# Gate-value products in PSUM, early weight operands and stored token operands in a fused attention and two-MLP kernel

## The chip, the cores and the metric

The kernel runs on one core of a Trainium2 chip. Its metric is the device time of one launch in microseconds, the median of several runs. Beside it stands the profiled execution, one run recorded by the hardware profiler; all rows below come from that one execution.

The engines are named as the profile names them: PE (TensorE, matmuls), PEld (its weight loads), DVE (VectorE), ACT (ScalarE), POOL (GpSimd) and SP (SyncE, here the queue that issues nearly all DMAs). PSUM is the memory that PE writes, eight banks of 128 partitions by 512 fp32 numbers; SBUF is the working memory, and DRAM lies behind the DMA queues.

## The reference, cut to what matters

```
state = 0                                     # a recurrence over 768 tokens, 4 batches x 8 heads, head size 48
y[t]  = r[t] @ (state + u * k[t] v[t]^T);  state = w[t] * state + k[t] v[t]^T
x  = y, laid out as 3072 tokens x 384
h  = max(x @ w1, x @ w2, x @ w3)              # first MLP, 384 -> 768
x  = h @ w_out                                # 768 -> 384
g, val = x @ w_gate, x @ w_val                # second MLP, 384 -> 1536, gated
out = (g * sigmoid(g) * val) @ w_out2         # 1536 -> 384
```

Everything is in fp32. The kernel reaches that accuracy with matmuls of the rounded type fp32r: each operand is split into a high and a low part, and one exact product is three matmuls (high x high, high x low, low x high; `mm3`, lines 618 to 621, and the loop in `product`, lines 926 and 927).

## The kernel before, in words

The 3072 tokens are six chunks of 512 (`NT`). The kernel has two halves.

First half: the attention of chunk c (24 units, `group` and its helpers) is computed beside the first MLP of chunk c-1 (`up`, `down`). PE does 18 `up` groups and three `down` results a chunk. The result goes to DRAM (`y1d`). The weights of the second MLP come in as 64-bit words and are turned to fp32 beside it (`bits`, chunks 8 to 19) and stored in `wfd`.

Second half, the gated MLP: three pairs of chunks (d = 0 to 2) times four quarters of the 1536 hidden features (q) make twelve units, n = 4d + q. A unit needs, for the gate (v = 0) and for the value (v = 1), the products of three weight blocks with three token blocks for two chunks, 18 block products; a fast scheme makes them from 15 (`ORD`, `CHAIN`). Each of the 15 is three matmuls of 128x128 by 128x512. So both operands are sums:

- token side, once a pair d: `y_sum` (POOL, 11 sums), `op_high` (ACT, rounding) and `op_low` (the remainder, DVE, for the indices in `SLOW` on POOL). The 15 results `op[d, r]` lie in one buffer each, so the operand i of the next pair can be written only when product i of the value side of the last unit of this pair has run.
- weight side, once a quarter q, in units 0 to 3: `w_sum` (POOL), `w_high` (ACT), `w_low` (DVE, parts of it POOL). The result is used at once and stored (`w_store`) for the units 4 to 11, which load it (`w_load`). The weights of the projection go the same way (`p_high`, `p_low`, `p_store`, `p_load`). Seven buffers `u0` to `u6` hold the parts in a ring (`WSLOT`).

What follows a product: PE accumulates into six PSUM chains (letters A to F in `CHAIN`; A and B use the two banks `gx`, the others a ring of four banks, `mm`). `snap` (ACT) copies a chain to SBUF, `join` (DVE) adds the chain's new state to such a copy, `mix` (POOL) adds two copies. After that `silu` (ACT, gate), `times` (DVE, gate by value, in SBUF), `prod_high` (ACT) and `prod_low` (DVE or POOL) give the operand of the projection. `proj` (PE, nine matmuls each, six a unit) uses two PSUM banks `po` and `collect` adds its result to an accumulator (ACT for the first quarter of a pair, else DVE). The six projections of unit n stand between the products of unit n+1 (`seq`, the table `gaps`: after products 10 and 13 of the gate side and 2, 6, 9 and 12 of the value side). A unit is 90 matmuls of products and 54 of projections.

The order of all work is made by a list scheduler (`Plan`), which gives each engine a fixed list from the costs, due times and dependencies written in the code; SP's list of DMAs comes out of the same plan. At run time each engine goes through its list in order and waits for what each entry needs. `close` (line 1044) marks the point at which the attention's buffers are given up and those of the second half come into being.

Of the kernel before, what the change touches and what calls it, by code (L numbers as in the profile page):

```python
# [20 lines left out]
C = 128  # L21
# [18 lines left out]
class Plan:  # L40
# [4 lines left out]
    SLOTS = 4  # L45
# [5 lines left out]
    def add(self, eng, cost, fn, deps=(), due=None, lat=0.1, slot=0, after=0.0, slack=0.0, kind=0):  # L51
        t = dict(kind=kind, eng=eng, cost=cost, fn=fn, deps=[d for d in deps if d is not None], due=due, lat=lat,
                 slot=slot, after=after, slack=slack, readers=[], id=len(self.items), start=None, end=None)
        self.items.append(t)
        return t
# [6 lines left out]
    def order(self):  # L62
# [21 lines left out]
        free, last, dma, slots, out = {}, {}, 0.0, [], []  # L84
# [3 lines left out]
        while avail:  # L88
            best = None
            for t in avail:  # L90
# [3 lines left out]
                if t["slot"] and len(slots) + t["slot"] > self.SLOTS:  # L94
                    held = [r for o, i in slots[-self.SLOTS:][:t["slot"]] for r, part in o["readers"] if part in (None, i)]
# [19 lines left out]
            t["end"] = t["start"] + t["cost"]  # L115
            free[t["eng"]] = t["end"]
# [3 lines left out]
            slots += [(t, i) for i in range(t["slot"])]  # L120
# [156 lines left out]
def fused(ctx: ExitStack, tc: tile.TileContext, pk, ub, wt_all, out):  # L277
# [10 lines left out]
           for q in range(NQ)]  # L288
    wpd = [dram.tile([128, 2, 9, C], F32, name=f"wpd{q}") for q in range(NQ)]
# [14 lines left out]
    psM = tail.enter_context(tc.tile_pool(name="psM", bufs=4, space=PSUM))  # L304
# [28 lines left out]
    for t, v in ((signs, 0.0), (small, 1.0), (tiny, -TINY), (blo, W_LO), (bhi, -W_HI), (one, 1.0)):  # L333
        nc.gpsimd.memset(t, v)

# [100 lines left out]
    def rk_sum(n):  # L436

        pas[n] = psM.tile([128, 8], F32, tag="mm", name="pa")
# [41 lines left out]
    def transposes(n):  # L480
        khT[n] = psM.tile([128, G, C], F32, tag="mm", name="kp")
# [228 lines left out]
    def up(c, f, m):  # L710
        ps = pss[c, f, m] = psM.tile([128, NT], F32, tag="mm", name="ps")
# [21 lines left out]
    def down(c, m, k):  # L733
        if k == 0:
            pss[c, m] = psM.tile([128, NT], F32, tag="mm", name="ps")
# [27 lines left out]
    def check_mat():  # L763
        pss["bad"] = psM.tile([1, 1], F32, tag="mm", name="ps")
        nc.tensor.matmul(pss["bad"], flags[:, 0:1], one, start=True, stop=True)

    def check_end():
# [11 lines left out]
            (2, (0, 0), 5, -1), (10, (0, 1), 13, -1), (8, (1, 0), (2, 0), 1))  # L779
    XTAG = {6: "r0", 14: "r1", 9: "r2", 11: "r0", 3: "xsh", 5: "r1", 7: "xsl", 13: "r2", 2: "r0", 10: "r1", 8: "r2"}  # L780
# [23 lines left out]
    def y_sum(d, r, one_, two, sign):  # L804
        ys2[d, r] = lptile([128, NT], F32, XTAG[r], "xr")
        nc.gpsimd.tensor_tensor(ys2[d, r], ys2[d, one_], ys2[d, two], ALU.add if sign > 0 else ALU.subtract)

# [13 lines left out]
    def p_words(q, tag):  # L821
        src = wfd[q].rearrange("p f (t c) -> p f t c", c=C)[:, :, 6:9, :]
        if tag:
            t = lptile([128, 3, 3, C], F32, tag, "wq")
            nc.sync.dma_start(t, src)
            wp_[q] = [t[:, f] for f in range(3)]
            return
        wp_[q] = []
        for f in range(3):
            t = lptile([128, 3, C], F32, Y_TAGS[f, 0], "wq")  # L830
            nc.sync.dma_start(t, src[:, f])
            wp_[q].append(t)

    WSLOT = {}
    free_slot = 6
    for n in range(3 * NQ):
        if n == 0:
            for e, (v, k) in enumerate((v, k) for k in range(3) for v in range(2)):
                WSLOT[0, v, k] = e
# [6 lines left out]
    def w_tile(n, v, k):  # L846
        W[n, v, k] = lptile([128, 2, NPART, C], F32R, f"u{WSLOT[n, v, k]}", "W")

    def w_sum(n, r):
        part, at = next((k, s.index(r)) for k, s in enumerate(SUMS) if r in s)  # L850
        if n and part < 2:
            if at % 2 == 0:
                st[n, part, at] = lptile([128, 2, 2, C], F32, Y_TAGS[part + at // 2, 1], "st")
            t = st[n, part, at - at % 2][:, at % 2]
        else:
            if at == 0:
                st[n, part] = lptile([128, 4, 2, C], F32, "st", "st")
            t = st[n, part][:, at]
# [7 lines left out]
    def w_pieces(n, v, k):  # L866
# [9 lines left out]
        if n and k < 2:  # L876
            sums = [(st[n, k, e][:, 0:min(2, NPART - at - e), v, :], slice(at + e, min(at + e + 2, NPART)))
                    for e in range(0, NPART - at, 2)]
        else:
            sums = [(st[n, k][:, 0:NPART - at, v, :], slice(at, NPART))]  # L880
        return [(src, t[:, 0, q, :], t[:, 1, q, :]) for src, q in raw + sums]

    def w_high(n, v, k):
        w_tile(n, v, k)
# [10 lines left out]
    def w_load(n, v, k):  # L895
        w_tile(n, v, k)
        nc.sync.dma_start(W[n, v, k].bitcast(F32), wsd[n % NQ][v, k])

    def p_high(n):
        W[n, "p"] = lptile([128, 2, 9, C], F32R, "up", "Wp")  # L900
        for f in range(3):
            nc.scalar.activation(W[n, "p"][:, 0, 3 * f:3 * f + 3, :], wp_[n][f], AF.Copy)

    def p_low(n):
        for f in range(3):
            h, l = (W[n, "p"][:, e, 3 * f:3 * f + 3, :] for e in range(2))
            nc.vector.tensor_tensor(l, wp_[n][f], h.bitcast(F32), ALU.subtract)
# [8 lines left out]
    def product(n, v, i):  # L916
        r, ch = ORD[i], CHAIN[i]
# [3 lines left out]
        elif first:  # L921
            X[n, v, ch] = psM.tile([128, NT], F32, tag="mm", name="py")
# [22 lines left out]
    def mix(n, v, k):  # L945
        if k == 5:
            b = sbuf(n, v, 5)
            (nc.gpsimd if n else nc.vector).tensor_tensor(b, buf[n, v, "d"], buf[n, v, "u"], ALU.subtract)
# [7 lines left out]

    def times(n, k):
        g = buf[n, 0, k]
        nc.vector.tensor_tensor(g, g, buf[n, 1, k], ALU.mult)  # L959

    FINALS = (5, 2, 0, 1, 3, 4)

    def prod_high(n, k):
# [8 lines left out]
        nc.scalar.activation(prod[n, k][:, 0, :], buf[n, 0, k], AF.Copy)  # L972
# [652 lines left out]
```

## Time and profile before

| what | value |
|---|---|
| median of 3 runs | 834.95 us (833.98 to 837.02) |
| the profiled execution, its time | 836.19 us |
| its span, first to last instruction | 834.3 us |
| PE busy | 791.7 us, 95% of the span |
| DVE busy | 659.3 us, 79% |
| ACT busy | 459.7 us, 55% |
| POOL busy | 325.4 us, 39% |
| mean granted TensorE clock | 0.974 of full |

A busy time is the union of an engine's instructions. Matmuls overlap in the pipeline, so a PE that shows as busy goes on issuing at the spacing of the matmuls' starts, and that spacing, not the length of one, is its cost. DVE and POOL instructions overlap a little at their ends too. An idle stretch of an engine is put down to what released it. [...]

### The profile page before, as it was taken

How to read it: one execution, taken by the hardware profiler on the slowest of the kernel's cores; microseconds unless marked ns; L12 is line 12 of the kernel's file. 1: busy time of each engine (PE TensorE's matmuls, PEld its weight loads, DVE VectorE, ACT ScalarE, POOL GpSimd, SP SyncE). 2: the span in 40 equal slices, each digit the busy share in tenths (PEclk: the TensorE clock that was granted, in tenths of full speed). 3: DMA queues.
4: the chain of work that ended last, by engine and by line, in shares of the span. 5: the costliest groups of instructions: out<-in, count | busy, mean ns of one | idle time of the engine just before them, and what ended most of it. 6: DMA issues, size and time to landing. Idle time of an engine off the chain costs nothing.

```text
span 834.3 us, 15790 instructions
## 1 busy us (share of the span) xinstructions
PE 791.7 (95%) x6140; PEld 643.1 (77%) x6140; DVE 659.3 (79%) x931; ACT 459.7 (55%) x997; POOL 325.4 (39%) x294
## 2 busy tenths in 40 slices
PE   6799999999999999999979899969999979999997
PEld 5688668888888888888767687758888857888885
DVE  7889999988979955378795998997476797846764
ACT  4643465564546562345756556645776875665440
POOL 1000344221232100349877786973322494322421
PEclk9699999999999999999998999989999999999999
DMA  9746465875575544441580758467666644645302
GB/s 278 217 153 216 124 169 152 208 255 137 139 239 143 173 146 145 165 186 70 212 300 31 271 213 292 152 249 270 237 233 216 264 178 159 247 155 209 118 1 80
DMA packets 41970, 154.44 MB, mean 185 GB/s; under 512 B 5632, under 2 KB 10624, under 8 KB 36896
## 3 DMA queue, kind: packets, MB, share of 16 engines
q1 hardware_dynamic: 41744, 153.23, 55.7%
q8 instruction: 50, 0.82, 0.4%
q14 instruction: 32, 0.26, 0.1%
q10 hardware_dynamic: 144, 0.13, 0.0%
HBM read 114.41 MB, written 36.96 MB: 181 GB/s over the span
## 4 chain that ended last, share of the span: by engine, by line
PE 80%; DVE 12%; issue 2%; POOL 2%; ACT 1%; DMA 1%; SPq 0%; DVEq 0%; POOLq 0%; ACTq 0%
PE px L927 12%; PE ps L619 11%; PE py L927 10%; PE ps L620 10%; PE ps L621 10%; PE po L619 5%; PE po L621 5%; PE po L620 5%; DVE sb L959 2%; PE ps L740 2%; PE y L509 2%; PE kp L483 2%; DVE yo L815 2%; PE sc L565 1%; PE sc L469 1%
## 5 line engine op out<-in xcount | busy, mean ns | idle before, releaser
L927 PE MATMUL px<-yo,W 128*128 128x512 f32 x519 | 137.2, 399 | 21.2 <-DVE yo L815 11.4
L927 PEld LDWEIGHTS px<-yo,W 128*128 128x128 f32 x519 | 98.2, 191 | 45.7 <-DVE sb L941 12.8
L619 PE MATMUL ps<-xh,hi 128*128 128x512 f32 x324 | 130.1, 401 | 1.4 <-DMA xh<-xsh 1.4
L620 PE MATMUL ps<-xl,hi 128*128 128x512 f32 x324 | 127.3, 393 | 0.0
L621 PE MATMUL ps<-xh,lo 128*128 128x512 f32 x324 | 127.2, 393 | 0.0
L951 POOL TENSOR_TENSOR sb<-sb 128x512 f32<-128x512 f32 x46 | 69.1, 1505 | 148.4 <-ACT sb L936 95.3
L927 PE MATMUL py<-yo,W 128*128 128x512 f32 x456 | 125.9, 396 | 0.7 <-DVE yo L815 0.5
L927 PEld LDWEIGHTS py<-yo,W 128*128 128x128 f32 x456 | 87.1, 191 | 20.0 <-DVE yo L815 0.9
L941 DVE TENSOR_TENSOR sb<-px,sb 128x512 f32<-128x512 f32 x95 | 63.7, 685 | 21.7 <-PE px L927 18.7
L619 PE MATMUL po<-pr,Wp 128*128 128x512 f32 x198 | 78.0, 394 | 0.0
L620 PE MATMUL po<-pr,Wp 128*128 128x512 f32 x198 | 77.6, 392 | 0.0
L621 PE MATMUL po<-pr,Wp 128*128 128x512 f32 x198 | 77.4, 391 | 0.0
L936 ACT ACTIVATE sb<-px 128x512 f32<-128x512 f32 x96 | 56.3, 597 | 35.0 <-PE px L927 31.5
L619 PEld LDWEIGHTS ps<-xh,hi 128*128 128x128 f32 x324 | 61.5, 190 | 14.8 <-issue 2.3
L383 POOL COPY total<-I 128x8 f32<-128x8 f32 x24 | 12.7, 530 | 151.9 <-DVE I L374 80.5
L723 DVE TENSOR_TENSOR hw<-hw,ps 128x512 f32<-128x512 f32 x60 | 40.8, 680 | 38.9 <-PE ps L621 26.6
L621 PEld LDWEIGHTS ps<-xh,lo 128*128 128x128 f32 x324 | 61.4, 190 | 13.0
L620 PEld LDWEIGHTS ps<-xl,hi 128*128 128x128 f32 x324 | 61.4, 190 | 12.2 <-issue 0.2
L995 DVE TENSOR_TENSOR acc<-po,acc 128x512 f32<-128x512 f32 x53 | 36.4, 687 | 39.2 <-PE po L621 37.9
L972 ACT ACTIVATE pr<-sb 128x512 fp32r<-128x512 f32 x70 | 42.8, 634 | 43.5 <-DVE sb L959 43.4
L959 DVE TENSOR_TENSOR sb<-sb 128x512 f32<-128x512 f32 x71 | 63.6, 919 | 0.3
L955 ACT ACTIVATE sb<-sb 128x512 f32<-128x512 f32 x72 | 44.4, 630 | 29.7 <-DVE sb L941 29.3
(187 smaller groups left out, 1669.9 us busy)
## 6 DMA issues: line engine op xcount, KB each, us to landing
raw<-wt SPq DMA_DIRECT2D x27, 1152.0 KB, 6.4
W<-wsd SPq DMA_DIRECT2D x48, 640.0 KB, 4.4
inpA<-pk SPq DMA_DIRECT2D x42, 294.0 KB, 5.3
wsd<-W SPq DMA_DIRECT2D x17, 640.0 KB, 4.8
Wp<-wpd SPq DMA_DIRECT2D x8, 1152.0 KB, 5.1
wfd<-fp32s SPq DMA_DIRECT2D x12, 576.0 KB, 3.4
inpT<-pk SPq DMA_DIRECT2D x16, 384.0 KB, 4.1
inpV<-pk SPq DMA_DIRECT2D x24, 200.0 KB, 4.7
```

Source lines behind the costliest of these rows:

```text
L619: nc.tensor.matmul(ps, lh, rh, start=first, stop=False)
L620: nc.tensor.matmul(ps, lh, rl, start=False, stop=False)
L621: nc.tensor.matmul(ps, ll, rh, start=False, stop=last)
L723: nc.vector.tensor_tensor(hws[f], hws[f], pss[c, f, m], ALU.max)
L927: nc.tensor.matmul(X[n, v, ch], w, x, start=first and k == 0, stop=k == 2, skip_group_check=True)
L936: nc.scalar.activation(sbuf(n, v, k), X[n, v, ch], AF.Copy)
L941: nc.vector.tensor_tensor(b, X[n, v, ch], b, ALU.add)
L951: nc.gpsimd.tensor_tensor(b, b, buf[n, v, "u" if k == 3 else "d"], ALU.add)
L955: nc.scalar.activation(b, b, AF.Silu)
L959: nc.vector.tensor_tensor(g, g, buf[n, 1, k], ALU.mult)
L972: nc.scalar.activation(prod[n, k][:, 0, :], buf[n, 0, k], AF.Copy)
L995: nc.vector.tensor_tensor(acc[a], t, acc[a], ALU.add)
```

## The change

- `times` writes the product of gate and value into PSUM (two banks by turns: the fourth bank of `mm`, and a new one, `pt`) in place of SBUF; `prod_high` and `prod_low` read it there. `prod_low` is always on DVE. All six of a unit are entered after the unit's last product, in the order 5, 2, 1, 3, 0, 4.
- For that the ring `mm` has three banks in the second half, and `po` one; the last two units' projections use banks of `mm` and `gx` besides. A projection is two pieces, six matmuls and three.
- The weights of unit 1 and then of unit 0 are made first, from `close` on, with two buffers for the sums (`st`, `q0`); unit 1 is stored and loaded again like the units from 4 on. The projection weights of units 1, 2, 0 and 3 are made in that order. The words of chunks 17 to 19 come in at a spacing of 11 in place of 21.5 (units of the plan). `p_low` is on POOL; `w_low` of units 2 and 3 is on DVE for the gate and on POOL for the value.
- The token sums of pairs 1 and 2 are made from about three units before the pair begins (due at `base - 100 + 8 * e`); six of the eleven go to DRAM (`xd`) and are loaded back before their use (due at `AT_X - 14`). `SLOW` has two entries (5 and 8) for pairs 1 and 2, six for pair 0 as before.
- The planner knows that DVE and POOL slow each other (`port`), has lower costs for DVE and ACT, and gives `snap` and `join` earlier due times (`SOON`).

```diff
@@ Plan.order
+            if t["port"]:
+                a, rate = (("POOL", 0.34), ("DVE", 0.76))[t["eng"] == "POOL"]
...
@@ buffers
+    xd = [{r: dram.tile([128, NT], F32, name=f"xd{d}{r}") for r in (3, 2, 7, 13, 10, 8)} for d in range(3)]
-    psM = tail.enter_context(tc.tile_pool(name="psM", bufs=4, space=PSUM))
+    psM = tail.enter_context(tc.tile_pool(name="psM", bufs=1, space=PSUM))
+    def mm(shape, name):
+        k = taken.get(ring_size[0], 0)
+        taken[ring_size[0]] = k + 1
+        return psM.tile(shape, F32, tag=f"mm{k % ring_size[0]}", name=name)
+    def x_store(d, r):
+        nc.sync.dma_start(xd[d][r], ys2[d, r])
+
+    def x_load(d, r, tag):
+        ys2[d, r] = lptile([128, NT], F32, tag, "xb")
+        nc.sync.dma_start(ys2[d, r], xd[d][r])
+    STAGED = (1, 0)
+    def st_tag(n, part):
+        return "st" if n not in STAGED else ("st", "q0")[(3 * STAGED.index(n) + part) % 2]
...
     def product(n, v, i):
+        ring_size[0] = 3
...
     def times(n, k):
-        g = buf[n, 0, k]
-        nc.vector.tensor_tensor(g, g, buf[n, 1, k], ALU.mult)
+        e = PORDER.index(k) % 2
+        gated[n, k] = (psO[0] if e else psM).tile([128, NT], F32, tag="pt" if e else "mm3", name="pt")
+        nc.vector.tensor_tensor(gated[n, k], buf[n, 0, k], buf[n, 1, k], ALU.mult)
...
-        nc.scalar.activation(prod[n, k][:, 0, :], buf[n, 0, k], AF.Copy)
+        nc.scalar.activation(prod[n, k][:, 0, :], gated[n, k], AF.Copy)
-        eng.tensor_tensor(prod[n, k][:, 1, :], buf[n, 0, k], prod[n, k][:, 0, :].bitcast(F32), ALU.subtract)
+        eng.tensor_tensor(prod[n, k][:, 1, :], gated[n, k], prod[n, k][:, 0, :].bitcast(F32), ALU.subtract)
...
@@ unit_words, p_steps
+        due = (SECOND + UNIT_T * n - 14) if n > 1 else {1: 358, 0: 380}[n] - 12
-                slow = n > 0 and v == 1 and k > 0
+                l = L["wl", n, v, k] = on("POOL" if n > 1 and v else "DVE", ...
+        due = SECOND + UNIT_T * (n + 1) + 3 if n == 3 else {1: 375, 2: 385, 0: SECOND + 5}[n]
+        slow = True
-    chunks = list(range(1, 8)) + steady + [("unit", q) for q in range(NQ)] + [("p", NQ - 1)]
+    chunks = list(range(1, 8)) + steady[:-1] + [("unit", 1), 19, ("unit", 0), ("p", 1), ("p", 2), ("unit", 2), ("p", 0), ("unit", 3), ("p", 3)]
...
-    SLOW = (4, 6, 8, 10, 12, 14)
+    SLOW = (5, 8)
+    SOON = 15.0
@@ operand sums
+            due = base - 100 + 8 * e if d else base - 12 + MM * ORD.index(r)
+            now = L["ys", d, r] = on("POOL", 1.35, y_sum, d, r, one_, two, sign)(deps, due, slack=1.0, after=due - 8 if d else 0.0)
+            if d and r in xd[d]:
+                L["xst", d, r] = dma(256e3, 1, x_store, d, r)([now], due + 5)
+                ld = L["xb", d, r] = dma(256e3, 1, x_load, d, r, tag)([L["xst", d, r]], AT_X[NQ * d, 0, i] - 14)
@@ finish, project
+        t = L["times", n, k] = on("DVE", 0.62, times, n, k)([j, L["silu", n, k]] + ([L["pl", *last_t[0]]] if len(last_t) > 1 else ...
-        slow = k in ((5, 2, 0) if n == NU - 1 else () if n % NQ == NQ - 1 else (5,))
+        slow = False
-        if turn > 1:
-            deps.append(L["collect", turn - 2])
+        elif ring == "po" and "po" in last_po:
+            deps.append(last_po["po"])
@@ loads
-        if n >= NQ:
+        if n not in (0, 2, 3):
```

## Rows read from the trace of the kernel before

**Rows 1.** The page, section 2: busy tenths of PE in 40 slices

```profile
PE   6799999999999999999979899969999979999997
```

**Rows 2.** PE timeline: start, length, engine, line, op, tiles, shape, count

```profile
402.07 1.52 PE L927 MATMUL px<-yo,tu 128*128 128x512 f32 x6
...
535.13 1.52 PE L927 MATMUL px<-yo,W 128*128 128x512 f32 x6
...
675.65 1.07 PE L927 MATMUL px<-yo,W 128*128 128x512 f32 x4
...
827.99 0.39 PE L621 MATMUL po<-pr,Wp 128*128 128x512 f32 x1
```

**Rows 3.** Table by stage: stretch, length, busy PE, PEld, DVE, ACT, POOL (count), PEclk, DMA, GB/s

```profile
402.07:535.13 133.06, 124.34 (x523) 100.40 (x522) 114.93 (x157) 86.41 (x178) 102.01 (x95) 0.96 0.56 205
535.13:675.65 140.52, 133.31 (x577) 108.97 (x576) 103.13 (x140) 92.52 (x160) 62.28 (x45) 0.98 0.66 236
675.65:828.30 152.65, 146.59 (x633) 119.05 (x631) 108.31 (x156) 80.02 (x150) 54.32 (x37) 0.98 0.42 147
```

**Rows 4.** The same table for single stretches of 20 us

```profile
420.00:440.00 20.00, 15.61 (x63) 12.27 (x62) 18.98 (x23) 10.88 (x21) 15.71 (x16) 0.90 0.79 292
480.00:500.00 20.00, 20.00 (x89) 16.54 (x88) 18.62 (x27) 11.01 (x27) 17.20 (x18) 0.99 0.55 206
540.00:560.00 20.00, 12.79 (x46) 9.20 (x45) 20.00 (x21) 7.08 (x13) 15.73 (x12) 0.83 0.66 247
680.00:700.00 20.00, 13.94 (x48) 9.99 (x48) 19.75 (x21) 10.26 (x20) 12.03 (x8) 0.83 0.33 122
```

**Rows 5.** DVE timeline, 422 to 431 us, then POOL timeline, 422 to 427 us

```profile
422.81 0.69 DVE L941 TENSOR_TENSOR sb<-py,sb 128x512 f32<-128x512 f32 x1
...
424.82 4.08 DVE L959 TENSOR_TENSOR sb<-sb 128x512 f32<-128x512 f32 x3
...
429.63 0.68 DVE L975 TENSOR_TENSOR pr<-sb,pr 128x512 fp32r<-128x512 f32 x1
430.24 0.67 DVE L943 TENSOR_TENSOR sb<-sb,py 128x512 f32<-128x512 f32 x1
...
422.75 1.18 POOL L890 TENSOR_TENSOR W<-st,W 128x256 fp32r<-128x256 f32 x2
...
424.29 1.76 POOL L890 TENSOR_TENSOR W<-st,W 128x512 fp32r<-128x512 f32 x1
```

**Rows 6.** PE and DVE timelines around 545 us

```profile
539.64 4.73 DVE L907 TENSOR_TENSOR Wp<-wq,Wp 128x384 fp32r<-128x384 f32 x3
...
548.50 1.22 PE L927 MATMUL px<-yo,W 128*128 128x512 f32 x2 [6.62 <-DVE yo L815]
...
551.23 0.63 PE L620 MATMUL po<-pr,Wp 128*128 128x512 f32 x1
```

**Rows 7.** Groups of DVE by line, 402 to 535 us: busy us, mean ns of one

```profile
L959 DVE TENSOR_TENSOR sb<-sb 128x512 f32<-128x512 f32 x18 | 20.1, 1149 | 0.0
L890 DVE TENSOR_TENSOR W<-ww,W 128x256 fp32r<-128x256 f32 (+1 forms) x16 | 11.7, 757 | 2.3 <-ACT W L886 2.3
...
L815 DVE TENSOR_TENSOR yo<-xr,yo 128x512 fp32r<-128x512 f32 x5 | 6.8, 1382 | 0.0
```

**Rows 8.** Last attention entry of DVE, then groups of POOL, 340 to 402 us

```profile
330.28 0.69 DVE L606 TENSOR_TENSOR xl<-y,xh 128x512 fp32r<-128x512 f32 x1 [0.23 <-ACT xh L586]
...
L863 POOL TENSOR_TENSOR st<-ww 128x256 f32<-128x256 f32 x9 | 9.5, 1065 | 6.7 <-DVE tu L890 5.6 <-DMA ww<-wfd 1.1
...
L806 POOL TENSOR_TENSOR xr<-y,y 128x512 f32<-128x512 f32 x4 | 6.3, 1577 | 2.8 <-DVE yo L815 2.8
```

**Rows 9.** PE and DVE timelines between two projections of a steady unit

```profile
619.89 1.52 PE L927 MATMUL px<-yo,W 128*128 128x512 f32 x6
...
620.49 0.68 DVE L995 TENSOR_TENSOR acc<-po,acc 128x512 f32<-128x512 f32 x1
...
621.93 0.39 PE L619 MATMUL po<-pr,Wp 128*128 128x512 f32 x1
```

More of the change, by code (lines that the diff above doesn't have):

```diff
@@ L83, in order @@
             t["due"] = min(dates)
-        free, last, dma, slots, out = {}, {}, 0.0, [], []
+        free, last, dma, out = {}, {}, 0.0, []
+        count, held_by = {}, {}
+        busy = {"DVE": [], "POOL": []}
         for t in items:
@@ L93, in order @@
                 ])
[L94 to L95 removed]
+                if t["slot"]:
+                    o = held_by.get(count.get(t["slot"], 0) % t["slot"])
+                    held = [r for r, part in o["readers"] if part in (None, 0)] if o else []
                     if any(r["start"] is None for r in held):
@@ L115, in order @@
             t["end"] = t["start"] + t["cost"]
+            if t["port"]:
+                a, rate = (("POOL", 0.34), ("DVE", 0.76))[t["eng"] == "POOL"]
+                at, left = t["start"], t["cost"]
+                for x, y in busy[a][-4:]:
+                    if y <= at:
+                        continue
+                    if x > at:
+                        if x - at >= left:
+                            break
+                        left -= x - at
+                        at = x
+                    if (y - at) * rate >= left:
+                        at, left = at + left / rate, 0.0
+                        break
+                    left -= (y - at) * rate
+                    at = y
+                t["end"] = at + left
+                busy[t["eng"]].append((t["start"], t["end"]))
             free[t["eng"]] = t["end"]
@@ L119, in order @@
                 t["end"] = max(t["end"], dma) + 1.0
-            slots += [(t, i) for i in range(t["slot"])]
+            if t["slot"]:
+                k = count.get(t["slot"], 0)
+                held_by[k % t["slot"]] = t
+                count[t["slot"]] = k + 1
             out.append(t)
@@ L875, in w_pieces @@
             raw = [(w[:, 1, 1:2, :], slice(0, 1))]
[L876 to L880, printed above, removed]
+        sums = [(st[n, k][:, 0:NPART - at, v, :], slice(at, NPART))]
         return [(src, t[:, 0, q, :], t[:, 1, q, :]) for src, q in raw + sums]
     def w_high(n, v, k):
-        w_tile(n, v, k)
+        w_tile(n, v, k, STAGE if n in STAGED else WSLOT)
         for src, h, l in w_pieces(n, v, k):
@@ L1022, in fused @@
     p = Plan()
+    SHARED = (y_sum, w_sum, op_low, w_low, mix, times, p_low, hidden, bits)
     def on(eng, cost, fn, *args):
-        return lambda deps=(), due=None, **k: p.add(eng, cost, lambda: fn(*args), deps, due, **k)
+        port = fn in SHARED and eng in ("DVE", "POOL")
+        return lambda deps=(), due=None, **k: p.add(eng, cost, lambda: fn(*args), deps, due, port=port, **k)
     def dma(size, count, fn, *args):
```

269 lines of the change are left out of this document (146 added, 123 removed).

## The prediction, made before the result was known

> **What bounds the kernel now.** I read the page's slices first: PE is at nine tenths or more nearly everywhere, and its low slices lie at the start (the first 40 us, attention before any MLP work), around slices 21 to 24 and in slices 27 and 34 [rows 1]. All but the start lie in the second half. So the question is how much PE time the second half loses, and to whom.
>
> The loss comes from PE's timeline. In an undisturbed unit, nine matmuls start from 619.89 to 621.93, so one costs 0.2267 us [rows 9]. The second half has 12 x 144 = 1728 matmuls, 391.7 us at that spacing. It starts at 402.07, and its last matmul starts at 827.99 and so gives PE free at 828.2 [rows 2]: 426.1 us, 34.4 lost. Unit 4 starts at 535.13 and unit 8 at 675.65 [rows 2], which splits the loss: units 0 to 3 (90 + 3 x 144 = 522 matmuls, 118.3 us) took 133.1, so 14.7 lost; units 4 to 7 (130.6 us) took 140.5, 9.9 lost; the rest (630 matmuls, 142.8 us) took 152.6, 9.8 lost. The counts of the table by stage agree with this [rows 3].
>
> Next, who causes it. In the table of 20 us stretches PE loses where DVE is at 18.98 to 20.0 of 20, and it loses nothing at 18.62 [rows 4]. So DVE is the bound there, and it decides from about 94% on. DVE is that full partly because of POOL. An instruction with both inputs in SBUF takes 1.36 us (4.08 for three) while POOL works on SBUF, and 0.68 alone; one with an input in PSUM stays at 0.69 while POOL works [rows 5]. Over units 0 to 3 `times` has a mean of 1.149 us and `op_low` of 1.382 [rows 7]. Back to back, clean ones start 0.61 us apart [rows 5]; I use that as their cost. After a long wait PE also runs at the lower level for a while: at 551.23 a matmul takes 0.63 us after the wait of 6.62, and the granted clock of that stretch is 0.83 [rows 4, 6]. So the 9.9 us are that wait and its after-effect, with some small waits.
>
> **The change part by part.** The base is the profiled execution: 836.19 us, with 1.9 us outside its span and 1.24 us above the median of 834.95.
>
> *Units 0 to 3, 14.7 lost.* Removed from DVE: about half of the weight remainders. One of the two groups of `w_low` has 16 instructions at 757 ns, 11.7 us [rows 7]; the other, of the sums, I take as large, 23 together. With units 2 and 3 alone left there, gate side only, 14 instructions at 0.757 = 10.6 us stay, so 12 us go. The projection's `p_low` goes to POOL (a group of three can cost 4.73 us [rows 6]); I count 4 us. `prod_low` gets cheaper by reading PSUM (0.61 in place of up to 1.36 when POOL is busy), but three of them come from POOL, so I book nothing. DVE's 114.9 us [rows 3] become about 99; the trace lists 18 `times` of 24 [rows 7], so I add 7: 106 of 118.3, or 90%, below the mark of 94%. POOL is no lighter: it loses a unit's sums to the first half but gains `p_low`, half of `w_low` and the 11 sums of pair 1 (1.58 us each while contended [rows 8]), so the 1.149 of `times` stays. Residual 3 us, between 0 and 7 (half of the loss).
>
> *The two changes of pair, 9.9 and 9.8 lost.* There DVE has, in one unit's length of 32.64 us, 16 joins, 6 `prod_low` and 6 `collect` at 0.61, 17.1 us; 6 `times` and now 13 `op_low`, which I take at 0.9, between 0.61 clean and 1.36 contended, since POOL is left with six `mix` and two `op_low`, under half of the time: 17.1 us. That is 34.2, of which two products' `times` and `prod_low` (2.9 us) may come later, as their projections do: 31.3, or 96%. This is at the mark, not far above it as now (20.0 of 20 with PE at 12.79 [rows 4]), where the sums of the new pair on POOL run beside it and `op_low` takes 1.382 [rows 7]. Those sums are now made and stored earlier; their loads are 12 more DMAs on SP. Residual 2 us each, between 0 and 5, so 4 in all.
>
> *Single bank `po`.* This is a wait the change adds: PE holds a projection until `collect` of the one before has ended, and all later products stand behind it. In a steady unit `collect` starts at 620.49 and ends at 621.17, and the next projection starts at 621.93 [rows 9]: 0.76 us to spare at the narrowest spacing (three products). At no stall it costs nothing; if two contended instructions of 1.36 [rows 5] stand ahead it is late by about 1 us. I take 1 us in all, up to 6.
>
> *Two banks for the products.* `times` waits on DVE for the `prod_low` two before it; behind it on DVE stand joins, for which PE waits. One round is `times`, `prod_high` and `prod_low`, some 0.61 + 0.58 + 0.61 with hand-overs (ACT's mean is 92.52 / 160 = 0.58 [rows 3]), two rounds in parallel. The first projection stands ten products, 6.8 us, after the unit's end and begins with two of the first three products: two rounds, about 5 us. Covered, bounds 0 to 3, counted in the last item. Writing a DVE result to PSUM is in no row; I take the 0.68 of reading it [rows 5], and 1.36 as the other end, already used for `times`.
>
> [...]
>
> *The weights made beside the first MLP.* The attention's last DVE entry ends at 330.97 and the first product is at 402.07 [rows 2, 8], so POOL has 71 us. Its work there at contended prices: 30 `w_sum` at 1.07 (32), 11 `y_sum` at 1.58 (17) [rows 8], six `op_low` at 1.76, the price of a remainder of 512 columns (11), two `p_low` of 1152 columns, scaled from it, at 4.0 (8): 68. At the cheapest POOL rows, 0.59 for 256 columns [rows 5], the same is 18 + 13 + 7 + 5 = 43. I take 56, between them: it fits. The second half's start moves by 0.5 us, between -0.7 (a small wait in the last `down` goes) and 5.
>
> *SP.* 24 stores and loads of operands and 8 more loads of weights enter its list. SP waits in order, so a load of weights behind a waiting store is late. No row shows this; I take 0, bounds 0 to 4.
>
> The first half keeps its matmuls; its order is planned anew with other costs: 0, plus or minus 1.5.
>
> The sum: 34.4 lost becomes 3 + 4 + 1 + 0.5 = 8.5, so 836.2 - 25.9 = 810.3 for a profiled execution, 809 against the median.
>
> **The rivals.**
> *The second half starts late.* For it: POOL idled before, waiting for DVE's `w_low` (5.6 us in one group [rows 8]), and the words of unit 0 can be loaded only when those of unit 1 are used up. With the 6.7 us of idle of that group the 68 become 75, 4 too many, and what is missing then are operands of the first products; with PE's lower level after the wait and a second such gap 4 to 9 us: 813 to 819. Against it: two buffers for the sums.
> *DVE stays the bound.* If `times` and `op_low` run at the contended 1.36, a change of pair needs 31.3 + 19 x 0.46 = 40 us, over 7 lost each, and units 0 to 3 lose 5 to 7: 816 to 826. For it: POOL's work in these units is not less. Against it: the planner now spreads it.
> *The single bank decides, slower.* If at each of the 50 close projections `collect` is late, the loss is 50 x the lateness: from 0.52 us on it eats the 25.9 us gained. With two contended instructions ahead (2.7 us, then 0.68, against 2.04 of spacing) it is 1.3 at worst, 0.7 in the middle: 50 x 0.7 = 35, so 844, range 835 to 865. Against it: the 0.76 us to spare, and DVE near 70% in steady units (103.13 of 140.52 even with a change of pair [rows 3]).
> *It doesn't do what it says.* The stalls only move: 831 to 839.
>
> **How the numbers follow.** Forecast 802 to 814: 0.58. Late start: 0.16. DVE still the bound: 0.15. No difference: 0.04. Slower: 0.07. The range of 8 in 10 starts at 801 (residuals of nearly zero) and takes in the first three cases up to 825. A measurement of this kernel tells 0.5% from no change, about 4 us: faster 0.89, same 0.03, slower 0.08 (the single bank's case, and a part of the stalls that move).
>
> **What would show it.** Right: in the profile after, PE at nine in slices 21 to 24, 27 and 34; `prod_low` near 0.68 with no mean near 0.9; no `op_low` near 1.38; unit 4 starting some 121 us after the first product. Wrong: waits of a projection for `collect`; a first product after 405; SP waits ahead of weight loads; DVE over 94% with PE waiting for joins.

## The result, and the profile of the changed kernel

The changed kernel takes 822.38 us (median of four runs, 819.86 to 822.74) against 835.99 (833.98 to 837.53) for the kernel before on the same chip: a ratio of 0.983, with a 95% interval from 0.980 to 0.986. The forecast was 809, with a range from 801 to 825. So sign and range held, and the size was 13 us too large: about half of the gain that was expected came.

The profiled execution took 822.74 us. Its page, section 2 (busy tenths of PE in 40 slices, and the granted clock):

```profile
PE   6799999999999999989998999989999999999997
...
PEclk9799999999999999998999999999999999999999
```

Of the low slices of [rows 1] between the start and the last one (21, 23, 27 and 33; the prediction's "34" is slice 33), three stand at nine now, and slice 27 at eight, where it was six. Two eights are new: slice 22 (431.0 to 451.6), where PE waits for a remainder at 439 to 441 (below), and slice 18, which ends at 369.5 and so lies in the first MLP; the clock is lower in the slice behind it. Then PE's timeline: the first product, units 4 and 8, the last matmul.

```profile
409.03 1.52 PE L959 MATMUL px<-yo,tu 128*128 128x512 f32 x6
...
534.39 1.30 PE L959 MATMUL px<-yo,W 128*128 128x512 f32 x5
...
671.54 1.29 PE L959 MATMUL px<-yo,W 128*128 128x512 f32 x5
...
814.83 0.39 PE L652 MATMUL po<-pr,Wp 128*128 128x512 f32 x1
```

Worked out as for [rows 2]: PE is free at 815.06, so the second half took 406.0 us and loses 14.3 over its 391.7, where 34.4 were lost before. But it starts 7.0 us later (409.03 against 402.07). 20.1 less 7.0 is the 13.1 that PE gains. The table by stage (columns as in [rows 3]) splits the 14.3 into 7.0 in units 0 to 3 (125.36 less 118.3), 6.6 in units 4 to 7 and 0.7 after that:

```profile
409.03:534.39 125.36, 120.65 (x524) 97.31 (x522) 99.23 (x135) 79.84 (x151) 90.92 (x82) 1.00 0.62 227
534.39:671.54 137.15, 133.39 (x578) 108.56 (x577) 105.27 (x145) 93.14 (x159) 54.84 (x38) 0.99 0.73 263
671.54:815.06 143.52, 143.52 (x633) 117.84 (x631) 102.39 (x163) 78.77 (x149) 32.68 (x24) 1.00 0.45 156
```

What PE waited for in the second half says most (waiter, what it waited for, us in total, times, longest). Before:

```profile
PE px L927 <- DVE yo L815: 11.4, 2, 6.6
PE px L927 <- DVE sb L941: 9.7, 6, 4.3
PE py L927 <- DVE yo L815: 0.5, 1, 0.5
PE py L927 <- POOL yo L815: 0.2, 1, 0.2
```

And in the changed kernel:

```profile
PE po L650 <- DVE acc L1036: 4.5, 4, 2.1
PE po L651 <- DVE pr L1011: 3.4, 4, 2.1
PE py L959 <- DVE yo L858: 0.3, 1, 0.3
PE py L959 <- DVE sb L973: 0.2, 1, 0.2
```

The waits for operands (`yo`) and joins (`sb`), 21.8 us, are down to 0.5. In their place stand two waits that the change itself adds: a projection waits 4.5 us for the single bank to be emptied (`collect`, L1036), and its second piece waits 3.4 us for the remainder of its last operand (`prod_low`, L1011).

One of each, from the timelines of DVE, ACT and PE. First the bank, at the first change of pair:

```profile
541.72 1.77 DVE L994 TENSOR_TENSOR pt<-sb 128x512 f32<-128x512 f32 x1
543.41 0.68 DVE L973 TENSOR_TENSOR sb<-px,sb 128x512 f32<-128x512 f32 x1
544.01 0.67 DVE L1036 TENSOR_TENSOR acc<-po,acc 128x512 f32<-128x512 f32 x1
...
544.74 0.50 PE L650 MATMUL po<-pr,Wp 128*128 128x512 f32 x1 [2.15 <-DVE acc L1036]
```

`collect` stands on DVE behind a `times` that takes 1.77 us and behind a join; PE starts as it ends. Then the remainder:

```profile
438.04 0.67 ACT L1008 ACTIVATE pr<-pt 128x512 fp32r<-128x512 f32 x1
...
438.41 1.70 DVE L923 TENSOR_TENSOR W<-ww,W 128x256 fp32r<-128x256 f32 x2
440.03 0.94 DVE L923 TENSOR_TENSOR W<-st,W 128x256 fp32r<-128x256 f32 x1
440.89 0.68 DVE L1011 TENSOR_TENSOR pr<-pt,pr 128x512 fp32r<-128x512 f32 x1
...
441.63 0.50 PE L651 MATMUL po<-pr,Wp 128*128 128x512 f32 x1 [2.07 <-DVE pr L1011]
```

ACT has the high part ready at 438.71, but DVE is in the middle of weight remainders until 440.97. DVE isn't full in either stretch (17.32 of 20 us at 540 to 560, 15.68 at 420 to 440): it is the place in a list that is worked off in order.

DVE's groups over units 0 to 3 (busy us, mean ns of one), to be read beside [rows 7]:

```profile
L994 DVE TENSOR_TENSOR pt<-sb 128x512 f32<-128x512 f32 x18 | 18.0, 1007 | 0.1
L1011 DVE TENSOR_TENSOR pr<-pt,pr 128x512 fp32r<-128x512 f32 x17 | 11.4, 678 | 0.2 <-ACT pr L1008 0.2
...
L858 DVE TENSOR_TENSOR yo<-xr,yo 128x512 fp32r<-128x512 f32 x6 | 7.0, 1191 | 0.0
```

Last, the late start. 6.3 us are lost in the last chunk of the first MLP, where the kernel before loses 1.0 (at 396 to 398); besides, that chunk starts some 1.6 us later (its first copy by ACT is at 355.96 against 354.34). PE, then DVE:

```profile
365.74 0.39 PE L652 MATMUL ps<-xh,lo 128*128 128x512 f32 x1
369.27 0.80 PE L650 MATMUL ps<-xh,hi 128*128 128x512 f32 x1 [3.15 <-DVE hw L754]
369.86 0.63 PE L651 MATMUL ps<-xl,hi 128*128 128x512 f32 x1
...
375.41 0.42 PE L652 MATMUL ps<-xh,lo 128*128 128x512 f32 x1
```

```profile
358.06 0.69 DVE L754 TENSOR_TENSOR hw<-hw,ps 128x512 f32<-128x512 f32 x1 [2.39 <-issue]
358.67 1.24 DVE L156 TENSOR_SCALAR fp32s<-raw 128x1152 int32<-128x1152 int32 x1
359.94 2.33 DVE L157 SCALAR_TENSOR_TENSOR fp32s<-raw,fp32s 128x1152 int32<-128x1152 int32 x1
362.31 2.35 DVE L158 SCALAR_TENSOR_TENSOR fp32s<-raw,fp32s 128x1152 int32<-128x1152 int32 x1
364.58 1.38 DVE L923 TENSOR_TENSOR tu<-ww,tu 128x128 fp32r<-128x128 f32 x1
...
367.29 1.34 DVE L728 TENSOR_REDUCE small<-raw 128x1 f32<-128x1152 f32 x1
368.55 1.27 DVE L754 TENSOR_TENSOR hw<-hw,ps 128x512 f32<-128x512 f32 x2
```

Between two joins of the MLP (`hw`, L754) DVE works for ten microseconds without a break: the sign words of raw chunk 19 (`bits`, L156 to L158), four weight remainders of unit 1 (L923), the size check (L728). PE waits 3.15 us for a join; then the next matmul starts 0.59 us after the first, and 13 more start 0.43 us apart in place of 0.2267: the lower level of the clock (granted 0.50 from 369.27 to 375.41, and 0.83 over 360 to 380), which costs 3.0 us more.

POOL has a share in those ten microseconds. It makes operand sums without a break from 359.25 to 365.81, and beside them L157 and L158 take 2.33 and 2.35 us; in the kernel before, the same sign step takes 1.35 at 367.73, where POOL is idle. The first remainder behind them (128x128, 364.58) takes 1.38, a later one of that shape 0.28. With the sign step L156 (1.24, against 0.75 before) that is some 3.5 us, as much as the wait; no run tells this share apart.

### The profile page after: what moved, and what is told of

Its sections match the earlier page's. It is cut to its first block, busy times and chain, and to the rows that moved or that the text cites. A ratio compares the mean times of both kernels' runs of the same rounds, so it can differ in the third digit from the quotient of the medians.

```text
span 821.0 us, 15809 instructions
## 1 busy us (share of the span) xinstructions
PE 788.6 (96%) x6140; PEld 641.3 (78%) x6140; DVE 653.5 (80%) x934; ACT 458.2 (56%) x983; POOL 295.3 (36%) x277
## 4 chain that ended last, share of the span: by engine, by line
PE 89%; DVE 6%; issue 2%; DMA 1%; ACT 1%; SPq 0%; DVEq 0%; ACTq 0%
PE px L959 15%; PE py L959 13%; PE ps L650 11%; PE ps L651 11%; PE ps L652 11%; PE po L651 6%; PE po L652 6%; PE po L650 6%; PE y L540 2%; PE ps L771 2%; PE kp L514 2%; PE sc L596 1%; PE sc L500 1%; DVE sb L973 1%; PE pa L471 1%
## 5 line engine op out<-in xcount | busy, mean ns | idle before, releaser
L959 PE MATMUL px<-yo,W 128*128 128x512 f32 x567 | 145.3, 391 | 0.1
L983 POOL TENSOR_TENSOR sb<-sb 128x512 f32<-128x512 f32 x46 | 66.0, 1435 | 193.1 <-ACT sb L968 133.4
L959 PE MATMUL py<-yo,W 128*128 128x512 f32 x498 | 134.5, 390 | 0.5 <-DVE yo L858 0.3
L959 PEld LDWEIGHTS px<-yo,W 128*128 128x128 f32 x567 | 106.8, 189 | 23.7 <-DVE sb L973 1.2
L959 PEld LDWEIGHTS py<-yo,W 128*128 128x128 f32 x498 | 93.1, 188 | 20.8 <-DVE yo L858 0.9
L650 PE MATMUL po<-pr,Wp 128*128 128x512 f32 x213 | 83.6, 392 | 4.5 <-DVE acc L1036 4.5
L651 PE MATMUL po<-pr,Wp 128*128 128x512 f32 x213 | 83.8, 393 | 3.4 <-DVE pr L1011 3.4
L652 PE MATMUL po<-pr,Wp 128*128 128x512 f32 x213 | 83.3, 391 | 0.0
L1008 ACT ACTIVATE pr<-pt 128x512 fp32r<-128x512 f32 x71 | 42.6, 601 | 57.7 <-DVE pt L994 55.3
L994 DVE TENSOR_TENSOR pt<-sb 128x512 f32<-128x512 f32 x71 | 69.5, 990 | 0.6
L414 POOL COPY total<-I 128x8 f32<-128x8 f32 x24 | 12.3, 514 | 159.3 <-DVE I L405 81.7
L1036 DVE TENSOR_TENSOR acc<-po,acc 128x512 f32<-128x512 f32 x53 | 36.3, 685 | 39.8 <-PE po L652 39.6
L754 DVE TENSOR_TENSOR hw<-hw,ps 128x512 f32<-128x512 f32 x60 | 40.7, 679 | 32.8 <-PE ps L652 15.9
L987 ACT ACTIVATE sb<-sb 128x512 f32<-128x512 f32 x72 | 43.9, 628 | 20.0 <-DVE sb L973 19.5
```

Source lines behind the costliest of these rows:

```text
L650: nc.tensor.matmul(ps, lh, rh, start=first, stop=False)
L651: nc.tensor.matmul(ps, lh, rl, start=False, stop=False)
L652: nc.tensor.matmul(ps, ll, rh, start=False, stop=last)
L754: nc.vector.tensor_tensor(hws[f], hws[f], pss[c, f, m], ALU.max)
L959: nc.tensor.matmul(X[n, v, ch], w, x, start=first and k == 0, stop=k == 2, skip_group_check=True)
L983: nc.gpsimd.tensor_tensor(b, b, buf[n, v, "u" if k == 3 else "d"], ALU.add)
```

## The experiments

Losses are worked out as above (the start of the first product, and PE's time after it over 391.7 us). Ratios are against the kernel before, on the same chip.

An edit lets the planner order everything anew, so each run shows the edit together with its new order. In four runs whose edits don't touch the first MLP (products_in_sbuf, products_one_bank, sums_at_change, collect_sooner) the first product still moves by 2.8 to 4.5 us; the waits that each run names say more of its cause than a difference of a few us.

| run | median us | ratio (95%) | first product | lost after it |
|---|---|---|---|---|
| changed kernel | 822.38 | 0.983 (0.980 to 0.986) | 409.0 | 14.3 |
| order_alone | 846.59 | 1.013 (1.010 to 1.015) | 401.2 | 45.9 |
| products_in_sbuf | 829.58 | 0.992 (0.990 to 0.995) | 406.0 | 22.7 |
| products_one_bank | 829.21 | 0.992 (0.989 to 0.995) | 405.5 | 23.2 |
| sums_at_change | 828.54 | 0.992 (0.990 to 0.994) | 404.5 | 21.5 |
| unit1_later | 829.78 | 0.993 (0.991 to 0.995) | 399.9 | 28.7 |
| collect_sooner | 822.00 | 0.984 (0.982 to 0.986) | 406.2 | 15.1 |
| late_bits | 819.71 | 0.983 (0.980 to 0.985) | 401.3 | 18.2 |
| late_bits_collect_sooner | 821.73 | 0.982 (0.977 to 0.986) | 401.3 | 21.7 |
| bits_sooner | 821.14 | 0.982 (0.980 to 0.984) | 401.3 | 20.2 |
| unit0_due_later | 822.31 | 0.983 (0.980 to 0.986) | 402.2 | 18.9 |
| mix_sooner | 827.15 | 0.989 (0.986 to 0.992) | 404.0 | 21.8 |
| words_other_buffer | 817.46 | 0.977 (0.975 to 0.978) | 402.8 | 15.9 |

**Is it the moved work, or only the planner's new numbers?** The kernel before, with the new costs and the rates of DVE and POOL when both run; two of its lines:

```diff
-            a = on("DVE", 0.69, join, n, v, k, ch, SIGN.get(i, 1))([t] + need, due + 1, slack=0.3)
+            a = on("DVE", 0.64, join, n, v, k, ch, SIGN.get(i, 1))([t] + need, due + 1, slack=0.3)
...
-        due += MM
+        due += MM - SOON
```

> The kernel before with only the planner's new numbers (costs of single operations, the slower rates of VectorE and GpSimd when both run, results due 15 us sooner): the same instructions on the same engines and banks as before, in another order. Theory, the moved work is what gains: 829 to 836, within 0.8% of the kernel before. Rival, the gain is the order's and the moved work adds little: 820 to 824, as the changed kernel.

846.6: both missed. The new order alone makes the old arrangement 11 us slower (in its waits 6.6 us are for operands from POOL, 5.3 for projection weights). So the new numbers gain nothing on the old arrangement. What they are worth with the moved work, no run shows: the moved work under the old numbers was not run.

**Part 1 undone.** Products in SBUF, two projection banks:

```diff
-        e = PORDER.index(k) % 2
-        gated[n, k] = (psO[0] if e else psM).tile([128, NT], F32, tag="pt" if e else "mm3", name="pt")
+        gated[n, k] = buf[n, 0, k]
...
-            t = po[n, c, m] = psO[0].tile([128, NT], F32, tag=ring, name="po", bufs=2 if ring == "gx" else 1)
+            t = po[n, c, m] = psO[0].tile([128, NT], F32, tag=ring, name="po", bufs=2)
```

> The changed kernel with its first part undone alone: products of gate and value go to SBUF, two PSUM banks for the projections, four for the ring, and VectorE's remainder of a product is SBUF-only again. Theory: the remainder costs VectorE some 0.25 us more in each of 70 (17 us in all, where VectorE is the bound only in a part of it), and the waits for the single projection bank and for the product banks (7.9 us of waits in the profile) go; the second half loses 16 to 18 us instead of 14.3 and the time is 823 to 827. Rival, the single bank and the two product banks cost more than they give: these waits go and nothing takes their place, the second half loses 7 to 10, and the time is 815 to 819.

829.6: slower by 7.2 us than the changed kernel, with intervals that don't touch. Waits for joins are back (3.9 us). The theory's direction held, its size was too small. DVE's group of `prod_low` in units 0 to 3:

```profile
L1010 DVE TENSOR_TENSOR pr<-sb,pr 128x512 fp32r<-128x512 f32 x17 | 16.5, 986 | 0.0
```

986 ns against 678 with the product in PSUM. Nor do the waits for a projection bank go: 4.8 us in two, with two banks.

**The banks dealt out the other way.** One bank for products, two for projections:

```diff
-        gated[n, k] = (psO[0] if e else psM).tile([128, NT], F32, tag="pt" if e else "mm3", name="pt")
+        gated[n, k] = psM.tile([128, NT], F32, tag="mm3", name="pt")
```

> The changed kernel with the banks dealt out the other way: one PSUM bank for the products of gate and value, two for the projections. Theory: the round of product, high part and remainder (0.61 + 0.6 + 0.68 and hand-overs, some 2.2 us) runs one at a time, six rounds are 13 us, longer than the 6.8 us ahead of the first projection, so projections wait for remainders in each unit; the waits for the sum of the projection before go: 827 to 833. Rival, the second projection bank is worth as much as the second product bank: 820 to 825.

829.2, as the theory said: projections wait 5.0 us for DVE's remainders and 3.0 for ACT's high parts, and none waits for its bank (3.1 us more are one wait for a weight remainder). It is 6.8 us slower than the changed kernel: the second bank is worth more to the products than to the projections.

**Part 3 undone.** The sums of pairs 1 and 2 made as their pair begins:

```diff
-        for e, (r, one_, two, sign) in enumerate(XPRE if d else XSUM):
+        for e, (r, one_, two, sign) in enumerate(XSUM):
```

> The changed kernel with its third part undone alone: the operand sums of pairs 1 and 2 are made as their pair begins, on GpSimd, with no round trip through DRAM, and six remainders of the operands on GpSimd. Theory: the changes of pair lose some 3 us more each, units 4 and 8 some 5 each, and the time is 826 to 830; the first product and units 0 to 3 stay as they are within 1 us. Rival, the gain of the changes of pair was that of VectorE's shorter list (products in PSUM): within 1.5 us of the changed kernel, 821 to 824.

828.5, the theory's case: 6.2 us slower, and waits for operands are back in PE's list:

```profile
PE px L959 <- POOL yo L858: 2.9, 2, 1.9
PE px L959 <- DVE yo L858: 2.5, 2, 1.3
PE py L959 <- POOL yo L858: 1.9, 1, 1.9
```

**Half of part 2 undone: unit 1's weights made beside unit 0.**

```diff
-    STAGED = (1, 0)
+    STAGED = (0,)
```

> The changed kernel with the weights of unit 1 taken out of the first MLP's end: they are made beside unit 0, half of their remainders on GpSimd, as those of units 2 and 3. Theory: VectorE was 36.1 of 40 us busy at 360 to 400 in the kernel before, and unit 1's remainders are 9 us more than fit there; without them the last chunk of the MLP has no stall, the first product is at 401 to 403 and no wait of over 1 us follows before 412. What unit 1 then loses by late weights comes on top: the second half loses 22 to 30 and the time is 824 to 832. Rival, it is only the place of the last sign words in VectorE's order: the first product stays at 407 to 409.

First product at 399.9, no wait in the MLP's last chunk and none up to 420: what delays the start is what unit 1's weights bring. That is more than their remainders: without them the sign words of chunk 19 come ten microseconds sooner too (L156 at 348.29 in place of 358.67), and POOL makes no sums of unit 1 there. So this run alone doesn't tell the load of DVE's list from its order, which was the rival. Without them early, PE waits 12.9 us for weights (7.3 for DVE's parts, 5.6 for ACT's), so the early weights are worth more than they cost: 7.4 us in sum.

The table for 360 to 400 us (columns as in [rows 3], DVE is the third engine) in the kernel before, in late_bits (below) and in unit1_later:

```profile
360.00:400.00 40.00, 39.28 (x173) 32.21 (x172) 36.13 (x43) 18.80 (x40) 31.14 (x25) 1.00 0.31 109
```

```profile
360.00:400.00 40.00, 40.00 (x178) 33.08 (x177) 39.00 (x43) 18.06 (x38) 32.04 (x26) 1.00 0.71 249
```

```profile
360.00:400.00 40.00, 40.00 (x178) 33.14 (x177) 33.33 (x36) 19.83 (x38) 32.58 (x23) 1.00 0.73 257
```

DVE had four microseconds free there. The weight remainders from 338 to 402 are 14 instructions and 11.7 us before, 28 and 23.3 us in late_bits; about 5 of the 11.6 us more lie ahead of 360. Tight as it is, it fits: in late_bits DVE is busy 39.00 of 40 us and PE loses nothing, while in the changed kernel PE stalls at 34.33 of 40. So the load makes the stretch crowded, and the order in it decides whether PE stands.

**The order inside that chunk.**

```diff
-                b = on("DVE", 0.67 if k == 0 else 1.28, bits, i, k)([b] + war, t0 + 14, slack=3.0 if k == 0 else 0.0)
+                b = on("DVE", 0.67 if k == 0 else 1.28, bits, i, k)([b] + war, t0 + (44 if i == 19 else 14), slack=3.0 if k == 0 else 0.0)
```

> The changed kernel with one edit: the due times of the last chunk's sign words, their store and their size check are 30 us later, so that in the last chunk of the first MLP VectorE takes the joins of the up products before them. Theory: the 6.3 us that the last chunk loses stand in VectorE's list; the gap of 3.1 us and the slow stretch behind it at 365 to 375 us go, the first product is at 402.5 to 404 instead of 409.0, and the time falls by 4.5 to 6.5 us, to 816 to 818. Rival, GpSimd's weight work of units 0 and 1 is what makes the last chunk late (the rival of the prediction, only through VectorE's slower operations): the joins still come late, the first product stays after 407 and the time falls by less than 2 us.

The stall is gone and the first product starts 7.7 us sooner: 6.3 are the stall, and the other 1.4 stand already in the chunk's start (its first copy at 354.56, against 355.96), ahead of the edit's place. The sign words hardly moved; one join came to stand ahead of L157, and that was enough:

```profile
357.27 1.12 DVE L156 TENSOR_SCALAR fp32s<-raw 128x1152 int32<-128x1152 int32 x1
358.64 0.69 DVE L754 TENSOR_TENSOR hw<-hw,ps 128x512 f32<-128x512 f32 x1 [0.25 <-PE ps L652]
359.25 2.21 DVE L157 SCALAR_TENSOR_TENSOR fp32s<-raw,fp32s 128x1152 int32<-128x1152 int32 x1
```

But the time falls by 2.7 us only, which the two intervals don't separate. 5.1 us are lost anew from 400 to 420. ACT there:

```profile
401.07 0.63 ACT L854 ACTIVATE yo<-xr 128x512 fp32r<-128x512 f32 x1 [4.06 <-POOL xr L842]
...
404.59 1.07 ACT L779 ACTIVATE y1s<-ps 128x512 f32<-128x512 f32 x2
```

ACT stands four microseconds at an operand's high part, whose sum POOL has not made; behind it wait the copies that empty the MLP's banks (`y1s`), and PE needs one of these banks for its first `py` (2.38 us of wait, until 405.22). A gap closed on one list opened on another.

**Less DVE work in that stretch.** Raw chunks due every 19.5 us:

```diff
-    STEADY = 21.5
+    STEADY = 19.5
```

> The changed kernel with the steady chunks of raw weights due every 19.5 us instead of 21.5, so that the sign words and the size check of the last chunk (7 us of VectorE) are done by about 345, where VectorE idles between joins. Theory, VectorE's load between 360 and 405 is what decides, not its order: with 7 us less there the first product is at 401 to 402.5, no wait of over 1.5 us follows before 412, the second half loses 13 to 16, and the time is 814.5 to 818. Rival, the run with the later sign words has shown all there is to gain: 819 to 821, with the waits at 402 to 409 still there.

821.1: the rival's case (0.1 above its range), though for a reason that neither named. The first product is at 401.3 as forecast, with DVE at 36.38 of 40, but ACT waits again, now for a load:

```profile
405.48 1.16 ACT L934 ACTIVATE Wp<-wq 128x1152 fp32r<-128x1152 f32 x1 [3.37 <-DMA wq<-wfd]
406.55 1.07 ACT L968 ACTIVATE sb<-px 128x512 f32<-128x512 f32 x2
```

The high part of unit 2's projection weights stands ahead of the copies of the first products; its words were asked for at 400.46 and ACT could start at 405.48. So with the sign words and the size check out of the way the MLP doesn't stall either; the 3 us behind it have another cause.

**Unit 0's weights due later** (`{1: 358, 0: 380}` becomes `{1: 358, 0: 392}`, chunks every 20 us, `collect` sooner):

> The changed kernel with chunks of raw weights due every 20 us, unit 0's weights due 12 us later and collect 20 us sooner. Theory: with VectorE's load between 360 and 405 at 36 of 40 the MLP's last chunk has no stall, and the operands of the first products now stand ahead of unit 0's remainders, so at most 1 us is lost from 400 to 412; 816 to 819. Rival, ScalarE again stands at the high part of a projection's weights while their words are on the way, as at 402 to 405 in bits_sooner: 820 to 823.

822.3, the rival: ACT waits 5.49 us for the same load, and PE 5.3 us behind it.

**That load taken out of the way.** bits_sooner, and besides another order of the raw buffers' users, with unit 0's projection weights due 10 us later:

```diff
-    chunks = list(range(1, 8)) + steady[:-1] + [("unit", 1), 19, ("unit", 0), ("p", 1), ("p", 2), ("unit", 2), ("p", 0), ("unit", 3), ("p", 3)]
+    chunks = list(range(1, 8)) + steady[:-1] + [("unit", 1), 19, ("unit", 0), ("p", 1), ("p", 2), ("p", 0), ("unit", 2), ("unit", 3), ("p", 3)]
...
-        return f"raw{k % 2 if k < 25 else 1}"
+        return f"raw{0 if k == 23 or k < 22 and k % 2 == 0 else 1}"
```

> The kernel of bits_sooner with one change: the words of unit 2's projection weights are read into the other of the two raw buffers, right behind those of unit 1, and those of unit 0 take their place; so no load is on its way when ScalarE comes to the high part of these weights, ahead of the first products. Theory, ScalarE's wait for that load (3.4 us at 402 to 405 in bits_sooner, 5.5 in unit0_due_later) is what held PE there, and with VectorE's load lowered nothing else is late: at most 1 us is lost from 400 to 420 instead of 3.3, and the time is 816.5 to 819. Rival, another list takes over (GpSimd's operand sums and remainders of the first pair): 2 to 4 us are still lost from 400 to 420, and the time is 820 to 823.

817.5, the theory's case. ACT and PE at the start of the second half:

```profile
403.03 0.60 ACT L779 ACTIVATE y1s<-ps 128x512 f32<-128x512 f32 x1 [1.38 <-PE ps L652]
403.71 1.28 ACT L968 ACTIVATE sb<-px 128x512 f32<-128x512 f32 x2
```

```profile
402.83 1.52 PE L959 MATMUL px<-yo,tu 128*128 128x512 f32 x6
404.19 1.52 PE L959 MATMUL py<-yo,tu 128*128 128x512 f32 x6
405.55 0.84 PE L959 MATMUL px<-yo,tu 128*128 128x512 f32 x3
```

The products follow each other without a gap up to 418; 1.6 us are lost from 400 to 420 (at most 1 was expected), nearly all in one wait for a copy by ACT (1.32 at 419.95). This version beats both kernels: its interval lies wholly below that of the change.

**The two waits that the change adds.**

```diff
-        L["collect", turn] = on(*eng, collect, n, c, m)([t] + war, due + 3 * MM + 2, slack=0.5)
+        L["collect", turn] = on(*eng, collect, n, c, m)([t] + war, due + 3 * MM + 2 - 20, slack=0.5)
```

> The changed kernel with one edit: the sum that empties the projections' bank (collect) is due 20 us sooner, so that VectorE and ScalarE take it before other work. Theory: of the 4.5 us in which a projection waits for its bank 2 to 4 go, and the after-effect on the granted clock at 547 goes with the wait of 2.15: 818.5 to 820.5. Rival, the joins that collect is put ahead of are waited for in its place: 822 to 824.

822.0, the lower end of the rival's range, and no change that the intervals show. The waits for the bank fall from 4.5 to 1.6 us, and waits for joins and for ACT's copies of products rise from 0.2 to 5.3 (3.2 and 2.1). Together with late_bits:

> The two edits of late_bits and collect_sooner together. Theory: they act in different stretches (360 to 410, and the projections), late_bits gained 2.7 against the changed kernel and collect_sooner 0.4, so 819 to 819.8. Rival, by the new order a wait of another kind comes in their place: 821 to 824. Better than both, if what made collect_sooner's gain small was the MLP's stall alone: 817 to 818.5.

821.7, with runs from 818.15 to 824.75: nothing more to be told than that they don't add up.

**POOL's list.** In bits_sooner PE waits 3.0 us at 454 for a join while POOL makes eight weight sums ahead of a `mix`. With all three `mix` due 8 us sooner (one is shown), chunks every 20 us and `collect` 20 us sooner:

```diff
-            L["mix", n, v, 4] = on("POOL", 1.35, mix, n, v, 4)([a, act[n, v, 5]], due + 4, slack=0.4)
+            L["mix", n, v, 4] = on("POOL", 1.35, mix, n, v, 4)([a, act[n, v, 5]], due + 4 - 8, slack=0.4)
```

> The changed kernel with chunks of raw weights due every 20 us, collect 20 us sooner and the three sums on GpSimd that feed joins (mix) 8 us sooner. Theory: GpSimd takes mix ahead of the eight weight sums that stood ahead of it at 447 to 454 in bits_sooner, and that wait of 3 us goes: 816 to 819. Rival, the weights of units 2 and 3 are late instead: 820 to 824.

827.2: both missed. PE waits 8.6 us for joins in it and again 2.7 in the MLP's last chunk. That stretch stays open: words_other_buffer still loses 4.4 us from 440 to 460.

## Why the prediction was right, and where it was off

- **Range and luck.** 822.4 lies inside 801 to 825, but above the forecast (802 to 814) and the late start (813 to 819), and 3 us below the range's upper end. By its number it falls to "DVE stays the bound" (816 to 826), which isn't what happened: waits for joins are 0.2 us. Two signs of being wrong came, a projection that waits for `collect` and a first product after 405. That the range held is owed to its width, made for the rivals: the terms below that were off (start, single bank, product banks, units 0 to 3, changes of pair) were all too small.
- **DVE as the bound, and the waits for joins and operands: right.** 21.8 us of these waits became 0.5. Undoing part 1 or part 3 brings some of them back.
- **The mark of 94%: not borne out.** It was read from four stretches of 20 us. In the kernel before PE also waits 0.97 us for a join with DVE at 18.31 of 20 (500 to 520), and in late_bits it loses nothing with DVE at 39.00 of 40 (360 to 400). The busy share says where to look; what holds PE is what stands ahead of the operation that it needs.
- **DVE's sum for units 0 to 3: one term too many.** It added 7 us for six `times` that it took for missing. The trace has all 72; those not in the stretch run after unit 4 begins. DVE took 99.2 us, as the sum had it without them (99).
- **`prod_low` from PSUM: right.** It was forecast near 0.68 with no mean near 0.9: 678 ns, and 986 where the product stays in SBUF.
- **Start of the second half: the step that failed.** The sum took +0.5, between -0.7 and 5; it is +7.0. The step added up POOL's work alone, 56 of 71 us, and asked whether POOL can do it. POOL did: it was 55.84 us busy from 338 to 409. What I left out is DVE: the moved weights have remainders there, some 12 us a unit, beside joins that PE needs, and the same views show DVE at 36.1 of 40 us from 360 to 400 before. Adding them up would have shown a crowded list, and not yet the stall: late_bits and bits_sooner run as many remainders without it. What the sum couldn't show is ten microseconds of other work between two joins. The rival of a late start had the place and, at 4 to 9 us, the size, but another mechanism (operands of the first products missing): the MLP's last chunk waits for DVE's list, in which a sign step takes 2.33 us beside POOL's sums, against 1.35 in the kernel before, where POOL is idle. POOL's own lateness came to light only when that list was put right (late_bits).
- **Single bank: mis-sized.** Taken at 1 us, up to 6; measured 4.5 in four waits. The margin of 0.76 us was read in a steady unit [rows 9]; all four waits lie in units 0 to 3 or near a change of pair, where a `times` of 1.72 to 1.79 us stands ahead of `collect`. The slower rival was far off: the bank is late four times, not fifty.
- **Two banks for the products: mis-sized.** "Covered, 0 to 3"; measured 3.4 in four. A round takes 2.3 us by the mean lengths of its steps (1007, 601 and 678 ns) where 1.8 was forecast, and weight remainders or joins may stand between its steps on DVE.
- **Units 0 to 3:** residual 3 forecast, 7.0 measured, at the upper bound; most of it is the two items above (4.4 us of waits, 5.2 as gaps between starts). Unit 4 starts 125.4 us after the first product, not 121.
- **The changes of pair:** 4 forecast, with the bank 5; measured 7.3 from unit 4 on, 5 of it from 540 to 560, where the bank's wait of 2.15 is followed, 1.6 us after its end, by matmuls at 0.43 us (granted clock 0.68 from 547 to 551).
- **SP, and the first half:** that SP waits in order shows in the changed kernel: it stands 3.3 us at a store (`outT`, L1048, issued at 690.96), and the load of weights behind it (L930) follows at 691.60; at 464.21 a load of `Wp` (L945) goes out after 12.3 us, and the load behind it (L862) at 464.63. But no wait of PE ends with a load of weights or operands from DRAM in the second half; as forecast. The first half ahead of the last chunk is some 1.6 us longer, where 1.5 either way was allowed; in late_bits, whose edit lies behind that point, it is 0.2, so most of it may come and go between executions.

In sum: 8.0 lost in the second half forecast, 14.3 measured (6.3 too few); 0.5 at the start forecast, 7.0 measured (6.5 too few). These two are the 13 us.

## What to carry to other kernels

When work is moved beside other work, add up every engine that the moved work uses, in the stretch it is moved to, and not only the one that issues most of it; then look, on each list there, at the longest run of other work between two operations that the bounding engine needs. When one wait on an in-order list is closed, look at the head of each other list at that place: here DVE's sign words, POOL's sums and a load that ACT waits for took turns in holding PE at the end of the first MLP and the first products, and only the version that cleared all three kept the gain. A margin read in a steady stretch says nothing of the crowded ones.

## What the runs showed of the hardware

- Written to PSUM, a DVE result cost `times` what it cost in SBUF: a median of 0.70 us (changed kernel) against 0.69 (before), with a shortest of 0.68 either way. `times` is slower beside POOL either way (1007 ns mean to PSUM, 1149 to SBUF before [rows 7]; 1.77 us at 541.72, with POOL busy from 541.21 to 544.61). So is `op_low`, the other one with both inputs in SBUF (1191 ns mean over six in units 0 to 3; 0.67 us at 538.22, where POOL is idle), while joins and `prod_low`, with one input in PSUM, stay near 0.68 (means 680 and 678 ns in units 0 to 3; the join at 543.41, beside the same work of POOL, takes 0.68).
- The wait of 3.15 us in the MLP's last chunk was followed by 13 matmuls 0.43 us apart (granted clock 0.50 from 369.27 to 375.41); the one of 2.07 us at 439 by spacings of 0.34 and 0.24 (granted clock 1.00 from 439 to 446). The one of 2.15 us at 542 was followed by six matmuls 0.23 to 0.33 us apart and then by 0.43 (granted clock 0.73 from 544.74 to 551). So the length of a wait alone didn't tell what came after it. The first cost 6.3 us, about twice its length.
- A load of 576 KB asked for at 400.46 let ACT start at 405.48 in bits_sooner, while the 16 DMA engines were 91% busy from 400 to 420: what stood behind it on ACT's list was late by that much.
